# A block-sparse attention with a top-2 mixture of experts: eight key blocks per query block in f32, another order of the expert units, and seven block products in five experts' first layer

## The chip, the core and the metric

The kernel runs on one core of a Trainium2 chip. The core has TensorE (PE: matmuls, with weight loads beside them, PEld), VectorE (DVE), ScalarE (ACT), GpSimd (POOL) and SyncE (SP, which here issues DMAs). They share SBUF; matmuls write to PSUM, which DVE and ACT read. Each engine works through its own list in order and waits on semaphores for the others. The metric is device microseconds of one launch, the median of some runs.

## What is computed

```python
# attention: q, k, v (4 batches, 8 heads, 768 rows, 64 wide); blocks of 32 rows, so 24 blocks
mask = np.abs(blk_i - blk_j) <= 1                                  # neighbours
mask = mask | (blk_i == 0) | (blk_j == 0) | (blk_i == 23) | (blk_j == 23)   # first and last: all
mask[qb block, kb block] = True for kb in sampled_blocks[qb]       # three drawn blocks each
attn = softmax(where(mask, q @ k.T / 8, -1e9));  out = attn @ v
# experts: x = out as (3072, 512); 8 experts, 512 -> 1024 -> 512
noisy = x @ w_gate + log1p(exp(x @ w_noise)) * noise
top2, weights = two largest of noisy, softmax over the two
out[token] += weight * (relu(x[token] @ w1[e]) @ w2[e])            # for both experts of a token
```

So a query block outside the first and last sees at most eight of 24 key blocks: three neighbours, three drawn, two at the ends.

## The kernel before

**Attention** (class Attention, lines 46 to 423) computes dense scores. Two heads of a batch are a group; a step is one head and one tile of 128 rows, 192 steps in all. q and k are split into a high and a low f16 half (ACT copies, POOL subtractions in `split`), turned by DMA transposes, and the mask stands in extra rows of the operands. Per step PE runs two matmuls of 384 columns for the row maxima (`max_mm`, L227), four of 384 for the scores (`exp`, L255 and L256), and 18 of 64 or 65 columns for the product with v (`av`, L288: v in three f16 parts). DVE takes the row maximum over 768 scores (`max_red`, L234) and splits the exponentials, which ACT writes as integers (L257), into f16 halves (`halve`, L262). `steps` writes out the order by hand: within a step the pieces stand in a fixed order, maxima run a few steps ahead (`lead`), the product with v three steps behind (`LA`). The router's small operations stand between them (`background`).

**Routing** (class Router) runs per batch after its last group: it finds the two experts of each token and writes token number and weight into a table of slots in DRAM by indirect DMA.

**Experts** (class Experts) work in units: one of 640 rows for expert 0 (tokens of the first three batches), one of 224 rows for expert 0 (last batch), then seven of 816 rows for experts 1 to 7. A unit's rows are gathered from DRAM (POOL), turned by DMA (SP), and go through two layers with every operand split in two f16 halves, so three matmuls for one product. The first layer is `mm1` (L816; eight blocks of outputs, each 24 matmuls of up to 408 columns), ACT and DVE write the high and low halves of relu (L821, L822). The second layer is `mm2` (L836, 24 matmuls of 512 columns for 128 rows; L845 and the transposition L855 for the rows left over), then `finish` (L864: weight times result plus the token's earlier row) and an indirect DMA to `out` (L866). Weights come in eight pieces of 512 KB per expert (`load_piece` on SP's queue) and are split by ACT and DVE (`split_piece`, L729 and L730). `out` is filled with zeros during attention (`fill_out`, on ACT's queue).

The main function's loop over units says which loads, gathers and splits stand behind which block. Nothing is scheduled by a planner: the order on every engine is that of the code.

## Time and profile before

| | us |
|---|---|
| median of three runs | 1052.07 (1046.19 to 1056.2) |
| the profiled execution, its own span | 1028.6 |
| PE busy | 891.4 |
| DVE busy | 563.1 |
| ACT busy | 377.1 |
| POOL busy | 355.9 |

The span runs from the first to the last instruction that the profiler saw; the times of the runs hold something around it. Busy times are sums over stages with different limits, so they are read stage by stage. A matmul's duration holds a fixed part that the next one hides; the distance between two starts is what one costs in a row of them. "Granted clock" (PEclk) is TensorE's clock as a share of the full one.

### The profile page before, as it was taken

What the parts mean: (1) busy time and instruction counts of PE and PEld (TensorE: products, weight loads), DVE (VectorE), ACT (ScalarE), POOL (GpSimd) and SP (SyncE); (2) the same over time, 40 slices, a digit from 0 to 9 for tenths busy, and PEclk for the clock granted to TensorE, in tenths of its full rate; (3) what the DMA queues carried; (4) which work ended last, traced back from release to release, by engine and by line L of the source; (5) the groups of instructions that cost most, each with busy time, mean ns of one, the idle gap of its engine ahead of it and who ended that gap; (6) DMA issues with size and microseconds to landing.
All of it is one profiled execution on the core that took longest, in us unless ns stands there. A gap on an engine that the chain in (4) does not pass through costs nothing. (4 is left out here: it accounts for less than half of the span.)

```text
span 1028.6 us, 20575 instructions
## 1 busy us (share of the span) xinstructions
PE 891.4 (87%) x8413; PEld 529.1 (51%) x8413; DVE 563.1 (55%) x1039; ACT 377.1 (37%) x754; POOL 355.9 (35%) x399
## 2 busy tenths in 40 slices
PE   3788897779878878997899999989989999899993
PEld 1465565556555545653645455545544544454551
DVE  7699989979988977464123333323323323233320
ACT  2466666556656645432113123122122221221200
POOL 3142322542255253333360251342512513512211
PEclk9899999999999999998999999999999999999997
DMA  8988986899989766736957376295494483653200
GB/s 183 182 171 183 219 196 159 154 164 179 182 178 167 144 133 145 200 85 176 165 130 199 109 174 184 90 196 168 131 184 141 124 214 104 182 144 110 69 34 33
DMA packets 238073, 156.40 MB, mean 152 GB/s; under 512 B 172577, under 2 KB 213793, under 8 KB 237968
## 3 DMA queue, kind: packets, MB, share of 16 engines
q1 hardware_dynamic: 206816, 91.45, 44.1%
q0 software_dynamic: 14256, 39.58, 13.2%
q10 hardware_dynamic: 16896, 23.95, 8.6%
q8 instruction: 68, 1.11, 0.5%
q14 instruction: 37, 0.30, 0.1%
HBM read 79.62 MB, written 26.32 MB: 103 GB/s over the span
## 5 line engine op out<-in xcount | busy, mean ns | idle before, releaser
L257 ACT ACTIVATE p<-pe 128x384 int32<-128x384 f32 x384 | 183.0, 491 | 152.8 <-PE pe L256 125.7
L822 DVE SCALAR_TENSOR_TENSOR hl<-ph,hh 128x408 f16<-128x408 f32 (+2 forms) x136 | 75.6, 560 | 211.2 <-ACT hh L821 177.0
L866 POOL DMA_INDIRECT out_dram<-y,mt x56 | 73.0, 1304 | 323.9 <-DVE y L864 196.4
L234 DVE TENSOR_REDUCE m<-pm 128x1 f32<-128x768 f32 x192 | 181.6, 948 | 1.4 <-PE pm L227 1.4
L821 ACT ACTIVATE hh<-ph 128x408 f16<-128x408 f32 (+2 forms) x136 | 66.2, 492 | 301.9 <-PE ph L816 210.2
L227 PE MATMUL pm<-k,q 88*128 88x384 f16 x384 | 98.5, 340 | 67.8 <-DVE m L234 42.6
L262 DVE TENSOR_SCALAR p<-p 128x1536 f16<-128x1536 uint16 x192 | 124.7, 650 | 45.9 <-ACT p L257 44.0
L288 PEld LDWEIGHTS <-p 128*128 128x128 f16 x3456 | 130.4, 100 | 25.8 <-issue 4.7
L255 PE MATMUL pe<-q,k 128*128 128x384 f16 x384 | 128.7, 335 | 7.7 <-ACT p L257 4.4
L256 PE MATMUL pe<-q,k 128*128 128x384 f16 x384 | 127.9, 333 | 6.7 <-DMA q<-qb 6.7
L288 PE MATMUL po<-vx,p 128*128 128x65 f16 x1152 | 125.3, 197 | 1.8 <-issue 1.4
L288 PE MATMUL po<-vb,p 128*128 128x65 f16 x1152 | 125.8, 196 | 0.9 <-issue 0.9
L288 PE MATMUL po<-vl,p 128*128 128x64 f16 x1152 | 125.5, 195 | 0.0
L836 PEld LDWEIGHTS <-hh 128*128 128x128 f16 x768 | 75.0, 98 | 93.8 <-issue 8.8
L864 DVE SCALAR_TENSOR_TENSOR y<-py,mt,pv 128x512 f32<-128x512 f32 x48 | 36.0, 751 | 153.9 <-PE py L836 145.0
L816 PE MATMUL ph<-xta,w1hb 128*128 128x408 f16 x512 | 110.9, 339 | 9.6 <-DVE hl L822 8.7
L816 PE MATMUL ph<-xtb,w1ha 128*128 128x408 f16 (+1 forms) x448 | 95.3, 334 | 14.2 <-DVE hl L822 12.3
L227 PEld LDWEIGHTS <-q 88*128 88x128 f16 x384 | 37.9, 100 | 122.1 <-issue 96.7
L816 PEld LDWEIGHTS <-w1ha 128*128 128x128 f16 x576 | 57.4, 100 | 52.9 <-issue 18.4
L836 PE MATMUL py<-w2ha,hh 128*128 128x512 f16 x192 | 73.9, 385 | 4.9 <-DVE y L864 3.9
L816 PEld LDWEIGHTS <-w1hb 128*128 128x128 f16 x512 | 50.2, 98 | 49.7 <-issue 12.3
L836 PE MATMUL py<-w2la,hh 128*128 128x512 f16 x192 | 73.8, 384 | 0.3 <-issue 0.3
(172 smaller groups left out, 1404.3 us busy)
## 6 DMA issues: line engine op xcount, KB each, us to landing
wraw<-in_moe_w_dram SPq DMA_DIRECT2D x64, 512.0 KB
q<-q SPq DMA_DIRECT2D x32, 192.0 KB
raw_v<-in_v_dram ACTq DMA_DIRECT2D x16, 384.0 KB
out_dram<-zero ACTq DMA_DIRECT2D x8, 768.0 KB
x_rows<-x SPq DMA_DIRECT2D x16, 384.0 KB
raw_k<-in_k_dram ACTq DMA_DIRECT2D x14, 384.0 KB
raw_q<-in_q_dram ACTq DMA_DIRECT2D x14, 384.0 KB
k<-k SPq DMA_DIRECT2D x17, 192.0 KB
```

The lines of the kernel that those rows point to most:

```text
L227: self.nc.tensor.matmul(pm[:, c, 0:384], r["q3"][0:K, h, t, :], r["k2"][0:K, h, 3 * c:3 * c + 3, :], start=True, stop=True)
L234: self.nc.vector.tensor_reduce(self.st[g]["m", h][:, t:t + 1], pm[:, :, 0:384], axis=AX.XY, op=ALU.max)
L255: nc.tensor.matmul(pe[:, 0:384], r["k1"][:, h, c, :], r["q1"][:, h, t, :], start=True, stop=False)
L256: nc.tensor.matmul(pe[:, 0:384], r["k2"][:, h, c, :], r["q2", h][:, t, :], start=False, stop=True)
L257: nc.scalar.activation(p32[:, t].rearrange("p t c -> p (t c)"), pe[:, 0:384], AF.Exp, scale=0.125)
L262: self.nc.vector.tensor_scalar(p.rearrange("p t c w -> p (t c w)"), p32.bitcast(U16).rearrange("p t c -> p (t c)"), HC, None, op0=ALU.mult)
L288: self.nc.tensor.matmul(o, p[:, t, :, w], v, start=first and i == 0, stop=last and i == 2, skip_group_check=True)
L816: nc.tensor.matmul(ph[:, b, 0:m], w[wt][:, kb, fs], r["xt"][:, kb, a, o:o + m], start=i == 0, stop=i == last)
L821: nc.scalar.activation(hv, ph[:, b, 0:m], AF.Relu)
L822: nc.vector.scalar_tensor_tensor(self.hl[:, f, o:o + m], ph[:, b, 0:m], 0.0, hv, op0=ALU.max, op1=ALU.subtract)
L836: nc.tensor.matmul(py, h[:, f, o], w[x][:, f, :], start=i == 0, stop=i == last)
L866: nc.gpsimd.indirect_dma_start(out=self.out, out_offset=bass.IndirectOffsetOnAxis(ap=r["mt"][0:m, c, 0:1], axis=0), in_=y[0:m], in_offset= ...
```

## The change

**Inputs** are laid out on the host: q and k turned (two heads on 128 partitions), v with its columns in groups of four, v's rows of each query block's neighbours side by side (`vw`), weights in the order of the new pieces.

**Attention** works on f32 without splits. A q item is one batch, one tile of 128 query rows and four heads; there are 48. For each query block of 32 rows (`j`) and each head its scores are one matmul of 32 rows by 192 key columns (three neighbours in place, three drawn blocks that POOL has copied beside them with a block number from a register), and one per head for the 64 columns of the two end blocks. The two heads of a pair sit on partitions 0 to 63 and 64 to 127, the four query blocks write to strips of 32 partitions. DVE takes maxima, ACT the exponentials, PE turns them in f32, DVE and ACT copy them out, and 32 matmuls of 68 columns multiply with v, whose rows SP loads by block number. Repeated blocks get weight zero through `known`. A g item takes the first and the last query block of two heads against all keys; there are 16. x is turned by PE (`turn_x`) and no longer by DMA.

**Order of units:** 640 rows for experts 0 and 1 (first three batches), then 224 rows for experts 1 and 0 (last batch), then 816 rows for experts 2 to 7. Units 0 and 2 write `out` without reading it. `fill_out` stands in unit 0's first layer, on SP's queue.

**Experts 3 to 7** compute the first layer from seven products of blocks in place of eight (`layer1_fast`, 28 products in four groups of seven): sums of weight blocks (`weight_sums`, DVE) and of row blocks (`row_sums`, `row_differences`, DVE) are formed one unit ahead, and the products are added on the way out of PSUM (ACT copies, DVE additions). PSUM has seven single banks in place of three pairs.

The core of the diff:

```diff
-    def exp(self, n, x):
-        nc.tensor.matmul(pe[:, 0:384], r["k1"][:, h, c, :], r["q1"][:, h, t, :], start=True, stop=False)
-        nc.tensor.matmul(pe[:, 0:384], r["k2"][:, h, c, :], r["q2", h][:, t, :], start=False, stop=True)
-        nc.scalar.activation(p32[:, t].rearrange("p t c -> p (t c)"), pe[:, 0:384], AF.Exp, scale=0.125)
+    def scores(self, it):
...
+            for kh in range(2):
+                for e in range(2):
+                    mm(s[kh][64 * e:64 * e + 64, 0:384], qg[h, 2 * i + e, :],
+                       kk[h, NB // 2 * kh:NB // 2 * kh + NB // 2, 2 * i + e])
...
+        for e in range(2):
+            p = 2 * f + e
+            for j in range(self.NJ):
+                blk = min(max(t * self.NJ + j - 1, 0), NB - 3)
+                for par in range(2):
...
+                    mm(s[par][32 * j:32 * j + 32, e, 0:192], q[head(par), p, 32 * j:32 * j + 32], w)
+        for e in range(2):
+            p = 2 * f + e
+            for par in range(2):
+                mm(s[par][:, e, 192:256], q[head(par), p, :], kk[head(par), 0:NB:NB - 1, p])
+    def soft(self, it):
...
+        for par in range(2):
+            nc.vector.tensor_reduce(m[:, par], s[par].rearrange("p (e c) -> p e c", e=2), axis=AX.X, op=ALU.max, negate=True)
+        for par in range(2):
+            for e in range(2):
+                nc.scalar.activation(p[:, 2 * e + par], s[par][:, 256 * e:256 * e + 256], AF.Exp, bias=m[:, par, e:e + 1])
+    def av(self, it):
...
+        for h in range(4):
+            for x, v in ((0, va), (1, vb)):
+                for j in range(self.NJ):
+                    nc.tensor.matmul(o[32 * j:32 * j + 32, h], d[:, h % 2, h // 2, x, 32 * j:32 * j + 32],
+                                     self.values(v[:, self.slot(t, j)], 4 * f + h), start=h == 0 and x == 0,
+                                     stop=h == 3 and x == 1, skip_group_check=True)
+    def prefetch_k(self, b, t):
...
+        v = self.numbers(self.ri, t, mybir.EngineType.Pool, self.NB - 1)
...
+        for j in js:
+            for n in range(3):
+                nc.gpsimd.tensor_copy(kk[:, self.row(t, j) + n], flat[:, bass.ds(v[j, n] * P, P)])
+    def prefetch_v(self, b, t):
...
+        nc.sync.dma_start(va[0:96, js[0]:js[-1] + 1, 0:HD], part(self.vw[b, t]))
...
+        for j in js:
+            for n, d in enumerate((va[96:128, j], vb[0:32, j], vb[32:64, j])):
+                nc.sync.dma_start(d[:, 0:HD], vv[bass.ds(v[j, n], 1)].rearrange("o p c -> (o p) c"))
-        self.units = [(0, 0, CA), (E, 0, CB)] + [(e, e, C) for e in range(1, E)]
+        self.units = [(0, 0, CA), (1, 1, CA), (E + 1, 1, CB), (E, 0, CB)] + [(e, e, C) for e in range(NH, E)]
+    def layer1_fast(self, u, hook):
...
+        for n, (g, p) in enumerate(PRODUCTS):
...
+            for s in range(2):
+                for wt, a in ((0, 0), (0, 1), (1, 0)):
+                    nc.tensor.matmul(o, w[:, wt, slot, s * P:s * P + P], mv(s, a), start=i == 0 and p in tail,
+                                     stop=i == 5, skip_group_check=True)
...
+            if p == 2:
+                tt(once[g], bc[:, 0:M], once[g])
+                self.high(g, 0, M, once[g])
+                later.append((g, 0, M, once[g]))
+            if p == 4:
+                tt(both[g][:, 0], bd[:, 0:M], both[g][:, 0])
+            if p in (5, 7) and {(g, 5), (g, 7)} <= seen:
+                tt(both[g][:, 1], ba[:, 0:M], both[g][:, 1])
```

Three places show what stands on the engines. First PE within a step of attention: the two score matmuls of one half, two for a maximum of a later step, and the first of the 18 with v (p are the exponentials, vx, vl and vb the parts of v). Before:

```order
L227 LDWEIGHTS q_1413
L227 MATMUL pm<-k_101,q_1413 128x384
L255 LDWEIGHTS k_913
L255 MATMUL pe<-q_1074,k_913 128x384
L256 LDWEIGHTS k_100
L256 MATMUL pe<-q_1636,k_100 128x384
L288 LDWEIGHTS p_1789
L288 MATMUL po<-vx_103,p_1789 128x65
L288 LDWEIGHTS p_1789
L288 MATMUL po<-vl_109,p_1789 128x64
```

One q item of the change (ps holds scores and then the turned p, kk the keys, ptr the turned p in SBUF; va holds neighbours and the first drawn block, vb the rest):

```order
L298 MATMUL ps<-r_ident,p 128x128 x8
L225 MATMUL ps<-kk_105,q 32x192 x16
L225 MATMUL ps<-kk_105,q 128x64 x4
L320 MATMUL po<-va_99,ptr 32x68 x4
L320 MATMUL po<-vb_102,ptr 32x68 x4
```

The L320 pair stands four times, once for each head; outputs are now strips of 32 partitions. In the built program each of these f32 matmuls but the transpositions is two weight loads and two matmuls, which the list does not show.

Second, DVE in attention. Before, about once a step:

```order
L262 TENSOR_SCALAR p_4721<-p_4691 128x1536
L234 TENSOR_REDUCE m<-pm 128x1
L543 RECIPROCAL r_iw<-r_w 128x48
L546 SCALAR_TENSOR_TENSOR r_r_4757<-r_w,r_u 128x48
L262 TENSOR_SCALAR p_4759<-p_4726 128x1536
```

and in the change, once a q item:

```order
L302 COPY ptr<-ps 128x512
L391 COPY r_xT<-po 128x1024
L271 TENSOR_REDUCE m<-ps 128x2 x2
L327 TENSOR_SCALAR rc<-po 128x4
L328 RECIPROCAL rc<-rc 128x4
L330 TENSOR_TENSOR xr<-po,rc 128x256
```

The conversion over 1536 is gone and the maxima are over 512 scores in place of 768; r_ names are the router's.

Third, DVE in an 816-row unit's first layer. Before it held little but the low halves (hl) of relu and some weights:

```order
L822 SCALAR_TENSOR_TENSOR hl<-ph,hh 128x408 x4
L730 SCALAR_TENSOR_TENSOR w2la<-wraw,w2ha 128x1024
L752 TENSOR_SCALAR gi<-mt 128x6
L752 TENSOR_SCALAR gi<-mt 48x1
L822 SCALAR_TENSOR_TENSOR hl<-ph,hh 128x408 x12
```

and in a fast unit of the change (ta and tc are the sums of products, pa, pc and pd the PSUM banks, xf the row sums of the next unit):

```order
L963 SCALAR_TENSOR_TENSOR hl<-tc,hh 128x816
L963 SCALAR_TENSOR_TENSOR hl<-ta,hh 128x408
L825 SCALAR_TENSOR_TENSOR w_9985<-wraw,w_9985 128x1024
L836 TENSOR_TENSOR xf<-xta 128x816
L980 TENSOR_TENSOR tc<-pd,tc 128x408
L963 SCALAR_TENSOR_TENSOR hl<-pa,hh 128x408
L836 TENSOR_TENSOR xf<-xta 128x816
L980 TENSOR_TENSOR tc<-pa,tc 128x408
```

Additions that free a PSUM bank now stand in one list with sums for the next unit.

## Rows read from the trace of the kernel before

**Rows 1.** The page: span and busy time of the engines.
```profile
span 1028.6 us, 20575 instructions
PE 891.4 (87%) x8413; PEld 529.1 (51%) x8413; DVE 563.1 (55%) x1039; ACT 377.1 (37%) x754; POOL 355.9 (35%) x399
```

**Rows 2.** Stretches: length, busy us (count) by engine, granted clock, DMA share, GB/s.
```profile
11.00:420.00 409.00, 333.93 (x4777) 227.71 (x4777) 355.96 (x679) 239.76 (x535) 154.93 (x191) 0.97 0.85 172
420.00:514.00 94.00, 79.44 (x585) 50.03 (x583) 39.24 (x103) 26.37 (x46) 36.08 (x46) 0.93 0.66 156
514.00:1012.00 498.00, 477.98 (x3056) 251.18 (x3054) 158.80 (x231) 106.95 (x167) 160.12 (x141) 0.99 0.53 140
1012.00:1028.60 16.60, 0.00 (x0) 0.00 (x0) 0.64 (x1) 0.00 (x0) 0.98 (x1) 0.65 0.05 19
...
405.00:420.00 15.00, 11.83 (x203) 9.09 (x200) 5.92 (x11) 7.41 (x19) 3.82 (x4) 0.89 0.93 202
```

**Rows 3.** Groups by line in attention (busy us, mean ns, idle before), PE's longest wait.
```profile
L234 DVE TENSOR_REDUCE m<-pm 128x1 f32<-128x768 f32 x192 | 181.6, 948 | 1.4 <-PE pm L227 1.4
L262 DVE TENSOR_SCALAR p<-p 128x1536 f16<-128x1536 uint16 x192 | 124.7, 650 | 45.9 <-ACT p L257 44.0 <-issue 1.0
L257 ACT ACTIVATE p<-pe 128x384 int32<-128x384 f32 x384 | 183.0, 491 | 152.8 <-PE pe L256 125.7 <-PE pm L227 7.5 <-remote 7.0
...
PE pm L227 <- DVE m L234: 42.6, 79, 1.6
```

**Rows 4.** Timeline of PE in the experts: start us, length us, engine, line, operation.
```profile
516.35 0.85 PE L816 MATMUL ph<-xta,w1hb 128*128 128x408 f16 x4
...
582.92 0.38 PE L836 MATMUL py<-w2hb,hh 128*128 128x512 f16 x1
583.14 0.38 PE L836 MATMUL py<-w2lb,hh 128*128 128x512 f16 x1
...
439.75 0.71 PE L816 MATMUL ph<-xta,w1ha 128*128 128x320 f16 x4
```

**Rows 5.** Timeline of PE and its weight loads in one step of attention.
```profile
203.10 0.74 PEld L288 LDWEIGHTS <-p 128*128 128x128 f16 x18
...
203.97 0.32 PE L256 MATMUL pe<-q,k 128*128 128x384 f16 x1
204.13 0.49 PE L227 MATMUL pm<-k,q 88*128 88x384 f16 x2
```

**Rows 6.** The f32 transposition: one instance in the timeline; durations ns min/median/max.
```profile
990.53 0.60 PE L855 MATMUL pr<-r_ident,yt 128*48 128x128 f32 x4
...
L855 PE MATMUL pr<-r_ident,yt x32: 272/273/273, 513.7 to 990.9; 128*48 128x128 f32 x28, 128*96 128x128 f32 x4
```

**Rows 7.** Groups by line and shape on DVE and ACT.
```profile
L822 DVE SCALAR_TENSOR_TENSOR hl<-ph,hh 128x408 f16<-128x408 f32 x112 | 64.8, 582 | 188.1 <-ACT hh L821 160.8 <-issue 27.3
L822 DVE SCALAR_TENSOR_TENSOR hl<-ph,hh 128x224 f16<-128x224 f32 x8 | 3.0, 390 | 14.6 <-ACT hh L821 8.1 <-issue 6.4
L305 DVE RECIPROCAL rc<-rc 128x6 f32<-128x6 f32 x32 | 5.8, 180 | 0.0
...
L849 ACT ACTIVATE yt<-py 128x192 f32<-128x192 f32 x7 | 2.3, 330 | 38.7 <-PE py L845 32.3 <-PE pr L937 6.4
```

**Rows 8.** POOL's groups by line and shape; one DMA issue on SP's queue.
```profile
L317 POOL TENSOR_TENSOR x<-xr,x 128x384 f16<-128x384 f32 x32 | 29.8, 931 | 22.4 <-ACT x L315 22.3
L647 POOL DMA_INDIRECT slots<-r_pay,r_sl x48 | 51.5, 1072 | 39.4 <-DVE r_ot L639 30.2 <-issue 7.7 <-DVE r_pay L636 1.2
...
1.70 0.42 SPq L330 DMA_DIRECT2D raw_q<-in_q_dram  x1
```

**Rows 9.** Timeline of PE in the first two units, with waits in brackets.
```profile
478.97 0.59 PE L836 MATMUL py<-w2ha,hh 128*128 128x512 f16 x1 [3.63 <-DVE y L864]
...
501.47 0.53 PE L816 MATMUL ph<-xtb,w1ha 128*128 128x224 f16 x2 [3.66 <-DVE hl L822]
```

More of the change, by code (lines that the diff above doesn't have):

```diff
@@ L36 @@
 CB = 224
-NV = E + 1
+NH = 2
+NV = E + NH
 OVT = 18
@@ L163, in vsplit @@
-    def vsplit(self, g, part):
-        nc, D = self.nc, self.D
-        r = self.st[g]
-        vh, vl, vb = r["v"]
-        vh, vb = vh[:, :, :, 0:D], vb[:, :, :, 0:D]
+        self.ps_g = pool(ctx, "ps_g", 1, space=PSUM)
+        ep = pool(early, "aeb", 1)
+        two = lambda n: ep if n == 2 else self.buf
+        J = self.NJ
+        self.va = [two(i).tile([P, J, self.HW], F32, name=f"va{i}") for i in range(3)]
+        self.vb = [two(i).tile([P, J, self.HW], F32, name=f"vb{i}") for i in range(3)]
@@ L587, in run @@
         nc.scalar.activation(ex, dl, AF.Exp)
-        for _ in range(self.YL if last else self.YN):
+        for _ in range(self.YL if last else self.YN + 8 * (b == self.B - 2)):
             yield
@@ L598, in run @@
                          skip_group_check=True)
-        for _ in range(self.HO):
+        for _ in range(self.HO if last else 0):
             yield
@@ L779, in gather_prev @@
         r = self.st["u", u]
-        for c in self.chunks(u):
+        for c in () if self.plain(u) else self.chunks(u):
             m = self.rows_of(u, c)
@@ L796, in rows_of, with layer1 @@
         return P if c < full else left
+    def layer1(self, u, hook):
+        nc = self.nc
+        self.hh = self.hp.tile([P, self.FB, C], F16, name="hh")
+        self.hl = self.hp.tile([P, self.FB, C], F16, name="hl")
+        if self.fast(u):
+            return self.layer1_fast(u, hook)
+        for n, f in enumerate(FORDER):
+            self.mm1(u, f)
+            hook(n)
     def mm1(self, u, f):
@@ L833, in mm2 @@
             i = 0
-            for f in range(self.FB):
-                for h, x in ((self.hh, "w2h"), (self.hh, "w2l"), (self.hl, "w2h")):
-                    nc.tensor.matmul(py, h[:, f, o], w[x][:, f, :], start=i == 0, stop=i == last)
+            for f in FORDER:
+                for h, x in ((self.hh, 0), (self.hh, 1), (self.hl, 0)):
+                    nc.tensor.matmul(py, h[:, f, o], w(f)[:, x], start=i == 0, stop=i == last)
                     i += 1
@@ L1025 @@
     ip = early.enter_context(tc.tile_pool(name="init", bufs=1))
-    zero = ip.tile([P, DM], F32, name="zero")
+    zero = rp.tile([P, 256], F32, name="zero")
+    nc.vector.memset(zero, 0.0)
     att.start(ip)
-    nc.gpsimd.memset(zero, 0.0)
-    at(18, router.blank_table, ip)
-    at(21, router.send_table)
-    att.steps(on_group, step)
+    at(7, router.blank_table, ip)
+    at(9, router.send_table)
+    att.steps(router, done, step)
     late.close()
     ex.open_right(right)
+    second = ExitStack()
@@ new lines, in do @@
+    def do(u, what):
+        e = ex.units[u][1]
+        while freed:
+            next_load(*freed.pop(0))
+        for op, *a in what:
+            if op == "h":
+                ex.high_piece(e + (a[0] < 4), a[0])
+            elif op == "l":
+                low(e + (a[0] < 4), a[0])
+            elif op == "s":
+                if u + 1 < nu:
+                    ex.weight_sums(e + 1, a[0])
+            elif op in ("g", "x"):
+                v = u + (1 if a[0] < 0 else 2)
+                c = abs(a[0]) - (a[0] < 0)
+                if v < nu and v > FAST:
+                    (ex.gather if op == "g" else ex.xpose)(v, c)
+            else:
+                {"rs": ex.row_sums, "rd": ex.row_differences, "rh": ex.row_high, "rl": ex.row_low}[op](u + 1, *a)
```

1215 lines of the change are left out of this document (694 added, 521 removed), and 5 rows, old and new, of the table BACK.

## The prediction

> **What bounds the kernel now.** The stages come first, from the table of stretches [rows 2]. The profiled execution (span 1028.6 us [rows 1]) has four parts: 11.0 us until matmuls run in numbers, attention to 420, the first two expert units (640 and 224 rows) to 514, seven units of 816 rows to 1012, and a tail of 16.6 us. The median of the runs shown is 1052.1 us, 23.5 above the span; I carry that difference over unchanged.
>
> In attention VectorE (DVE) is busy 356 of 409 us and TensorE (PE) 334. The grouped lines name DVE's work: 192 row maxima of 948 ns and 192 conversions of 650 ns, 306 us; PE's longest wait there is for such a maximum, 42.6 us in 79 waits [rows 3]. So DVE holds attention, with PE close behind. In the seven expert units PE is busy 478 of 498 us and DVE 159: PE holds them, 498 / 7 = 71.1 us each.
>
> What a matmul costs is read from distances between starts, since matmuls overlap. Four of 408 columns take 0.85 us and one lasts 0.33, so starts are 0.171 apart; 512 columns 0.215, 320 columns 0.137 [rows 4]. That is one column per cycle of 2.4 GHz; the fixed 0.17 us of each duration is hidden in a row of matmuls. Weights of 128 columns load every 0.041 us (18 in 0.74 [rows 5]). The one f32 work on PE is the transposition of yt: four of 128 columns in 0.60, one lasts 0.273, so 0.109 apart [rows 6]: two cycles a column.
>
> **Attention after.** The dense scores, row maxima and conversions go. Now 48 q items (four heads, 128 queries, eight key blocks of 32 for each query block) and 16 g items (first and last query block against all keys) run, all in f32. In the built program an f32 product is two weight loads and two matmuls, one for either half of the weights; a transposition is one of each. No row shows such a product. Bounds: one pass at the transposition's two cycles a column, or two such passes. I take two, as the program has them: 192 columns cost 2 x 0.160 us.
>
> The second unknown weighs more. Consecutive matmuls now use different rows or columns of the array (heads on partitions 0 to 63 and 64 to 127, outputs in strips of 32). No row of before has two of them on the array at once; all its matmuls use 88 rows or more. Bounds: nothing overlaps, or all do. I take the middle case: both passes of one matmul need the same part of the array and the engine's order is kept, so a matmul's second pass lies beside the next one's first, and n matmuls cost n + 1 passes in place of 2n. Per batch (without overlap in brackets):
> - scores: 12 items x 17 passes x 0.160 = 32.6 us (12 x 32 x 0.160 = 61.4)
> - keys of the end blocks: 8 passes with 128-column weights, by the loads 8 x 0.041 = 0.33, x 12 = 4.0 (5.1)
> - transpositions of p: 12 x 8 x 0.109 = 10.5 (same)
> - product with v: 32 matmuls of 68 columns, 33 passes x 0.057, x 12 = 22.6 (43.8)
> - g items: 4 x (5 x 0.320 + 8 x 0.109) = 9.9 (13.7); their product with v 65 x 0.057 = 3.7 (7.3)
> - transpositions of x in f16, by DMA before: 48 x 0.055 = 2.6 (same).
>
> Sum 85.9 us a batch (144.4), four batches 344, the router's 56 matmuls a batch about 7 in all. The start stays at 11: the first g item needs the keys of one batch, 1.57 MB, 9 us at the 172 GB/s of [rows 2]. Attention ends at 11 + 344 + 7 = 362 in place of 420: -58.
>
> The Trainium skill, page "TensorEngine Tiling (Array Packing)", section "Tiling Modes", says that a change of tile shape drains the engine. By it, 62 changes a batch at the hidden 0.17 us would add 43 us. The trace does not settle it: an 88-row matmul follows a full one 0.16 later, without a gap [rows 5], and no smaller shape ran. The forecast leaves it out.
>
> What else must stay under PE's 85.9 / 12 = 7.2 us an item? DVE: reading PSUM costs 0.157 us + 1.04 ns an element (582 ns at 408, 390 at 224 [rows 7]). Two maxima of 512: 1.38; ptr copy 0.69; norm 0.18 + 0.18 [rows 7] + 0.42; half a turned x 0.61; a third of a g item 0.65; the router, an estimate of 30 us in all, 0.6. That is 4.7. ACT: four exps of 256 at 0.39 (330 ns at 192, 491 at 384 [rows 3, 7]), a copy 0.60, high 0.39: 2.6. POOL, per tile of two items (14.4 us): a scaling 1.2, two low 1.2, table writes 2.1, and eleven copies of 128 columns between nearly nothing and the 0.93 of a 384-column subtraction [rows 8]: 4.6 to 14.8; the copies are a third as wide, so I take 8. SP: 13 v loads and four more issues at 0.42 [rows 8], 7 us a tile. Without this cover each us over 14.4 would cost 24 us. DMA: v 34.6 MB, q, k and the rows of x 6.3 each, 53.5 MB in 351 us is 152 GB/s, below the 172 moved now. All hidden.
>
> **Expert units after.** At full rate 816 rows cost 192 x 0.171 (first layer, two halves of 408) + 144 x 0.215 (second) + 96 x 0.020 (the 48 rows left over) + 0.4 = 66.1 us, where 71.1 was measured: 5.0 lost a unit. A unit of 640 costs 192 x 0.137 + 120 x 0.215 = 52.1; one of 224 about 96 x 0.093 + 24 x 0.215 + 96 x 0.040 + 0.4 = 18.3. Before, these are 70.4 where 94.0 was measured, so 23.6 lost, among it waits of 3.6 us for y and 3.7 for hl [rows 9] and a clock of 0.93 [rows 2]. After there are two of each, 140.8. The last batch's routing now has 104 us of cover and not 52, but the zero fill of out (6.3 MB) has moved from attention into unit 0, ahead of weights on SP's queue. I take 15 lost: bounds 5 (a full unit's), and 32 (12.6 MB of fills, weights and rows at 202 / 0.93 = 217 GB/s [rows 2] need 58 us where the first layer takes 26).
>
> Then one plain unit, 71.1, and five fast ones. Seven block products for eight: 28 x 6 = 168 matmuls of 408 in place of 192, 24 x 0.171 = 4.1 less, 67.0 each. Their DVE work grows, by the formula above: sums from PSUM 12 x 0.58, lows 8 x 0.58 + 4 x 1.0, weights 4 x 1.22 + 4 x (0.96 + 1.22), weight sums 16 x 0.42, row sums and differences 12.3, y 5.3: 53 us a unit where 159 / 7 = 23 stood. It fits under 67 by little; I take no loss. Sum 140.8 + 15 + 71.1 + 335 = 562, before 592: -30.
>
> **Sum.** 362 + 562 + 16.6 = 940.6, plus 23.5 = **964 us**, own range 930 to 1000.
>
> **Rivals.**
> - Changes of tile shape cost a drain each, 4 x 62 x 0.17 = 43 more: 1007. For it: five shapes alternate in every item. Against: nothing in the rows. Chance 0.20. (The Trainium skill's rule in "TensorEngine Tiling (Array Packing)", section "Tiling Modes", is this one; no run here shows it.)
> - The fast units wait for DVE. In their first layer DVE has 26 us of work within 28.9 and stands between the PSUM banks and PE. If each loses 8: 40 more, 1004. Chance 0.09.
> - More overlap, or a cheaper f32 pass: PE falls below DVE. 4.7 x 48 = 226 us at the 0.87 share that DVE reaches now [rows 2] is 260, attention ends near 274: 876. Chance 0.13.
> - Slower: matmuls on different parts of the array do not overlap. Attention ends at 4 x 144.4 + 18 = 596: 1198. For it: nothing in the trace runs two at once. Against: the program alternates the parts. The point that decides: with the rest as above, attention must end before 450, 108 us a batch, so 62% of the assumed overlap is needed. Chance 0.12.
> - Slower: the clock. It was 0.97 in attention, 0.93 in the broken stretch to 514 [rows 2]. If narrow f32 matmuls ran at the lower level of 1.2 GHz, 344 would double: 1308. Chance 0.04.
>
> That the change doesn't do what it says is no rival: the dense steps are gone from the program.
>
> **How the numbers follow.** Forecast 0.42, drains 0.20, DVE 0.09, more overlap 0.13, no overlap 0.12, clock 0.04. The range 870 to 1060 holds the first four with their spread and leaves out the last two and some edges. A measurement of this kernel tells about 1% from no change. Faster by over 1% (below 1041): 0.41 + 0.15 + 0.06 + 0.13 = 0.75; within 1%: 0.01 + 0.04 + 0.02 = 0.07; slower: 0.01 + 0.01 + 0.16 = 0.18.
>
> **What would show it.** PE's starts within an item's scores 0.16 apart per matmul: the forecast; 0.32: no overlap; under 0.1: more overlap. Gaps of 0.1 to 0.2 us ahead of each change of shape: drains. The first expert matmul near 362, fast units 67 us apart, PE waiting for tc, ta or hl under 3 us a unit. The prediction is wrong in its reasons if PE is idle over a tenth of attention, or if DVE is the busier engine there.

## The result and the profile after

The changed kernel takes 918.87 us (median, 910.61 to 930.65) against 1051.28 (1046.19 to 1056.2) for the kernel before, run beside it: a ratio of 0.8758, 95% interval 0.8671 to 0.8845. (The run of 930.65 us came in a slower state of the core, and the ratio leaves it out.) The forecast was 964 us, range 870 to 1060. So the direction and the range held, but the point lies 45 us too high, outside the 930 to 1000 that the forecast gave its own mechanism and about as far from it as from its rival "more overlap" (876). Several of its steps were wrong, two of them in ways that cancel. The profiled execution took 920.24 us with a span of 918.2.

The page of the changed kernel, its head, beside [rows 1]:

```profile
span 918.2 us, 25196 instructions
...
PE 825.8 (90%) x10119; PEld 520.8 (57%) x10119; DVE 538.0 (59%) x1151; ACT 357.5 (39%) x666; POOL 381.3 (42%) x662
...
q8 instruction: 81, 1.33, 0.7%
```

The last line is one of the DMA queues: 81 packets, 1.33 MB, so 16 KB each. It returns below.

Stretches of the changed kernel, with the columns of [rows 2]: attention, the two units of 640 rows, the two of 224, the plain unit of 816, the five fast units, the tail.

```profile
14.00:353.67 339.67, 286.87 (x6485) 218.37 (x6486) 201.85 (x565) 168.07 (x373) 171.96 (x470) 0.90 0.71 170
353.67:462.30 108.63, 107.49 (x680) 62.94 (x680) 44.39 (x111) 27.69 (x51) 34.22 (x44) 0.98 0.71 206
462.30:511.50 49.20, 43.26 (x442) 34.99 (x441) 12.80 (x35) 10.36 (x22) 16.36 (x15) 0.90 0.59 143
511.50:586.67 75.17, 69.42 (x438) 36.11 (x436) 45.20 (x67) 21.34 (x31) 35.38 (x26) 0.95 0.76 182
586.67:902.14 315.47, 315.23 (x2062) 167.04 (x2060) 224.89 (x335) 125.12 (x185) 119.02 (x92) 1.00 0.53 143
902.14:918.20 16.06, 0.00 (x1) 0.00 (x0) 0.75 (x1) 0.00 (x0) 0.98 (x1) 0.64 0.06 20
```

Attention ends at 353.67 where it ended at 420 [rows 2] (forecast 362). The experts take 548.5 us to the last matmul (forecast 562; 592 before). The five fast units are 63.0 us each, PE busy without a break. DVE, which held attention before, is busy 202 of 340 us there. PE is the busiest, but idle 53 of 340, and its granted clock is 0.90 there.

PE's waits in attention, 14 to 350 us (total, times, longest):

```profile
PE po L320 <- issue: 23.9, 43, 2.4
PE ps L225 <- issue: 6.3, 6, 3.5
PE pog L346 <- issue: 6.3, 14, 1.3
PE po L390 <- DVE xe L369: 4.1, 4, 2.0
PE po L662 <- DVE xr L330: 4.0, 3, 1.9
```

36.5 of 53 us are "issue": PE stands in the middle of a row of matmuls and waits for nothing that the profile names. Here is one undisturbed q item, PE's timeline (start, length):

```profile
150.49 1.09 PE L298 MATMUL ps<-r_ident,p 128*128 128x128 f32 x8
151.51 1.47 PE L225 MATMUL ps<-kk,q 64*32 64x192 f32 x40
152.92 0.33 PE L320 MATMUL po<-va,ptr 128*32 128x68 f32 x8
153.06 0.30 PE L320 MATMUL po<-vb,ptr 128*32 128x68 f32 x8
153.18 0.30 PE L320 MATMUL po<-va,ptr 128*32 128x68 f32 x8
```

All 40 score passes are through in 1.41 us (152.92 - 151.51), and eight passes with v start every 0.12 us, so 64 in 0.94. Transpositions, scores and product come to about 3.4 us, 162 us for 48 q items; attention, with 16 g items, the turned x and the router's matmuls, takes 340. The item just ahead shows one reason:

```profile
147.49 0.30 PE L320 MATMUL po<-va,ptr 128*32 128x68 f32 x8
147.81 0.33 PE L320 MATMUL po<-vb,ptr 128*32 128x68 f32 x4
148.55 0.22 PE L320 MATMUL po<-vb,ptr 128*32 128x68 f32 x1 [0.41 <-issue]
149.28 0.22 PE L320 MATMUL po<-vb,ptr 128*32 128x68 f32 x1 [0.51 <-issue]
150.01 0.28 PE L320 MATMUL po<-vb,ptr 128*32 128x68 f32 x2 [0.52 <-issue]
```

The product with v, 0.94 us when it runs through, takes 3.3 us here, in bursts 0.73 us apart. So attention has far less work than the forecast gave it, and loses time in a way that the forecast did not hold.

**Two patterns of stalls.** I counted PE's recorded instructions (matmuls, weight loads and the semaphore instructions between them) from the first one on. In the first 100 us the three longest waits without a named releaser stand behind number 1216, 1728 and 1984; in other executions behind 704, 2240, 2752, 3264, 4544, 4800. The differences are multiples of 256, on all three chips named below. Of these instructions 20412 are on record, and the instruction queue brought 81 packets: one per 252. So a block of 16 KB holds 256 of PE's instructions, and these are waits for the next block. The packets' own times agree: with the changed kernel on the quick chip (below) 14 of the 15 such waits of over 0.4 us in attention, 24.4 us, end 1.2 to 1.6 us after a packet of this queue has landed. In the first profile it is 11 of 47, 13.7 us. The second pattern is the train above: short bursts 0.7 us apart. It has another place: 37 of those 47 waits begin within 2.3 us after one of the 36 writes by which POOL fills the slots in attention (L716), and such times are 19% of attention (a few waits count for both).

### The profile page after: what moved, and what is told of

The parts are those of the page before. It is cut to its first block, busy times and chain, and to the rows that moved or that the text cites. A ratio compares the mean times of both kernels' runs of the same rounds, so it can differ in the third digit from the quotient of the medians.

```text
span 918.2 us, 25196 instructions
## 1 busy us (share of the span) xinstructions
PE 825.8 (90%) x10119; PEld 520.8 (57%) x10119; DVE 538.0 (59%) x1151; ACT 357.5 (39%) x666; POOL 381.3 (42%) x662
## 3 DMA queue, kind: packets, MB, share of 16 engines
q0 software_dynamic: 13760, 38.01, 13.2%
q8 instruction: 81, 1.33, 0.7%
## 4 chain that ended last, share of the span: by engine, by line
PE 81%; issue 6%; DVE 6%; another core or an unknown queue 2%; ACT 1%; DMA 1%; POOL 0%; SPq 0%; DVEq 0%; POOLq 0%
PE pc L1038 27%; PE ps L225 10%; PE pa L991 9%; PE po L320 7%; PE ps L298 5%; PE pa L952 5%; PE pd L991 5%; PE pd L952 3%; PE pc L1047 3%; PE pog L346 2%; PE pc L991 2%; DVE m L271 2%; PE ps L286 2%; PE po L390 1%
## 5 line engine op out<-in xcount | busy, mean ns | idle before, releaser
L1038 PE MATMUL pc<-w,hh 128*128 128x512 f16 x768 | 229.5, 380 | 0.0
L1038 PE MATMUL pc<-w,hl 128*128 128x512 f16 x384 | 146.0, 380 | 0.0
L991 PEld LDWEIGHTS <-w 128*128 128x128 f16 x840 | 82.2, 98 | 63.1
L274 ACT ACTIVATE p<-ps,m 128x256 f32<-128x256 f32 x192 | 75.2, 474 | 73.7 <-DVE m L271 63.8
L271 DVE TENSOR_REDUCE m<-ps 128x2 f32<-128x512 f32 x96 | 61.9, 684 | 49.8 <-PE ps L225 42.9
L225 PE MATMUL ps<-kk,q 64*32 64x192 f32 (+1 forms) x1920 | 75.9, 333 | 7.1 <-issue 6.3
L894 POOL DMA_INDIRECT xg<-x_rows,gi x56 | 69.9, 1249 | 23.4 <-issue 15.0
L320 PE MATMUL po<-va,ptr 128*32 128x68 f32 x1536 | 61.5, 237 | 16.8 <-issue 12.7
L186 POOL COPY kk<-kk 128x128 f32 x264 | 64.6, 295 | 28.2 <-PE ps L225 21.6
L825 DVE SCALAR_TENSOR_TENSOR w<-wraw,w 128x1024 f16<-128x1024 f32 (+1 forms) x58 | 65.2, 1126 | 18.9 <-ACT w L821 18.9
L320 PE MATMUL po<-vb,ptr 128*32 128x68 f32 x1536 | 63.4, 234 | 11.5 <-issue 11.2
L716 POOL DMA_INDIRECT slots<-r_pay,r_sl x48 | 48.7, 1014 | 39.2 <-DVE r_pay L705 27.3
L320 PEld LDWEIGHTS po<-va,ptr 128*32 128x32 f32 x1536 | 41.5, 115 | 31.0 <-issue 19.2
```

Source lines behind the costliest of these rows:

```text
L186: nc.gpsimd.tensor_copy(kk[:, self.row(t, j) + n], flat[:, bass.ds(v[j, n] * P, P)])
L225: mm = lambda o, l, r: nc.tensor.matmul(o, l, r, start=True, stop=True, skip_group_check=True)
L271: nc.vector.tensor_reduce(m[:, par], s[par].rearrange("p (e c) -> p e c", e=2), axis=AX.X, op=ALU.max, negate=True)
L274: nc.scalar.activation(p[:, 2 * e + par], s[par][:, 256 * e:256 * e + 256], AF.Exp, bias=m[:, par, e:e + 1])
L320: nc.tensor.matmul(o[32 * j:32 * j + 32, h], d[:, h % 2, h // 2, x, 32 * j:32 * j + 32], self.values(v[:, self.slot(t, j)], 4 * f + h), st ...
L825: self.nc.vector.scalar_tensor_tensor(lo, t, WS, hi, op0=ALU.mult, op1=ALU.subtract)
```

## The experiments

Three chips took part, and the kernel before ran at 996.44, 1036.06 and 1051.95 us (medians) on them; I call them the quick, the middle and the slow one. Which chip gave the first result above is not on record; the times of the kernel before beside it are those of the slow one. Comparisons in microseconds are made on one chip, or say so. On the middle chip the kernel before spread over 1028.66 to 1044.28 us and the four ratios carry no verdict; the changed kernel itself did not run there, and the readings rest on the traces.

**Without v's traffic** (middle chip).

```diff
     def prefetch_v(self, b, t):
...
+        if b * self.T + t >= 3:
+            return
...
```

> The loads of v after the first three tiles are left out (30 of 34.6 MB), with whatever waits for them; the product with v reads what the three buffers hold, so its numbers are of other rows. The changed kernel's attention runs from 14 to 350 us; in it TensorE is idle 51 us, 36.5 of them in rows of matmuls that wait for nothing the profile names (issue), in bursts of a few matmuls with 0.4 to 0.7 us between. Theory A, instructions: the profile's instruction queue carries 81 blocks of 16 KB against 20238 matmuls and weight loads, one per 250, and such a block comes late while v is on the DMA engines: the issue waits fall from 36.5 to under 8 us and attention ends by 320, the whole 30 or more shorter. Theory B, late v: the same gain, but by v itself. Theory C, the chain of an item (PE, DVE maximum, ACT exponential, PE) sets the pace: attention ends at 340 or later whatever the issue waits do, since other waits take their place.

Measured: 888.22 us (886.08 to 892.12), ratio to before 0.8619 [0.8568, 0.8669]; attention ends at 328.8, with 22.3 us of issue waits left.

**v loaded but not read** (middle chip). `av` and `global_av` read buffer 0; the loads go to buffers 1 and 2.

```diff
-        va, vb = self.st["v", b, t]
+        va, vb = self.va[0], self.vb[0]
...
```

> All loads of v are made, but into two buffers that nobody reads; the product with v reads a third one, loaded once, so its numbers are of other rows and nothing waits for a later load. Theory A (instruction blocks come late behind the traffic of v): the issue waits stay near 36 us and attention ends at 343 to 360. Theory B (v itself is late): as without loads, attention ends by 320. Theory C: no change, ends at 340 to 355 with the issue waits as they come.

Measured: 911.45 us, 0.8834 [0.8777, 0.8891]; attention ends at 344.1, issue waits 34.1. So with the traffic but without any wait for v, the stalls are all there; without the traffic attention is 15 us shorter. That speaks for the traffic (A) and against late v (B) and a chain that sets the pace whatever happens (C). But theory A had named under 8 us and an end by 320, and 22.3 us stay without traffic, mostly trains: A is not all. Sorted by place, the waits of over 0.4 us that end after a packet landed fall from 16.3 to 2.1 us when v is not loaded; of the 24 that are left 20 stand behind POOL's writes.

PE's waits with v not loaded (its lines stand two further down):

```profile
PE po L322 <- issue: 16.9, 34, 1.1
PE pog L348 <- issue: 4.6, 14, 0.5
```

None is longer than 1.1 us now: the long block waits are gone, the short bursts are not.

**Same part of the array in a row** (middle chip). The loops change places, so that eight products of one strip follow each other in the product with v, and two of one part in the scores.

```diff
...
-        for h in range(4):
-            for x, v in ((0, va), (1, vb)):
-                for j in range(self.NJ):
+        for j in range(self.NJ):
+            for h in range(4):
+                for x, v in ((0, va), (1, vb)):
```

> The same matmuls in another order: consecutive score matmuls (two heads pairs of one block) and consecutive products with v (eight of one block) now use the same part of the array, where the change alternates the parts. In the changed kernel 40 score passes take 1.41 us and 64 passes with v 0.95 us an item. If the overlap comes from alternating parts: 32 x 0.160 + 0.33 = 5.4 us and 64 x 0.057 = 3.6 us, and 48 items make attention some 150 to 310 us longer, the span 1070 to 1230. If passes overlap whatever part they use: 1.4 and 0.95 as now, span within 10 of 918. The forecast's own model (a second pass beside the next matmul's first) would lie at 3.0 and 1.9 with alternating parts, and gives the long version here.

Measured: 958.94 us (958.52 to 959.35), 0.9291 [0.9233, 0.935]; attention ends at 396.8. One item of it:

```profile
143.74 1.53 PE L225 MATMUL ps<-kk,q 64*32 64x192 f32 x40
145.20 0.31 PE L320 MATMUL po<-va,ptr 128*32 128x68 f32 x2
145.34 0.28 PE L320 MATMUL po<-vb,ptr 128*32 128x68 f32 x2
145.46 0.28 PE L320 MATMUL po<-va,ptr 128*32 128x68 f32 x2
145.57 0.28 PE L320 MATMUL po<-vb,ptr 128*32 128x68 f32 x2
...
145.93 0.31 PE L320 MATMUL po<-va,ptr 128*32 128x68 f32 x4
...
148.27 0.28 PE L320 MATMUL po<-vb,ptr 128*32 128x68 f32 x2
```

With v, two passes start every 0.117 us where eight did: 0.0585 a pass, no overlap within a strip, against the 0.057 of the forecast's formula. Only where one strip follows another do passes overlap (the rows of four), so the whole product takes 3.13 us where it took 0.94. So the overlap of the change is fourfold and comes from the four strips alternating. The scores did not slow down: two products in a row in one part, with eight parts in turn, still take 1.46 us. That half of the expectation was wrong; what order of the scores would break their overlap was not tried.

More telling is the total. 48 items x 2.2 us is 106 us more work on PE, but attention ended only 53 us later than with v unread on this chip (and not 150 to 310). PE's idle time fell from 52 to 22 us, issue waits among it from 34.1 to 10.9 with a single one left behind a packet, and the clock rose from 0.93 to 0.99: a slower PE hardly outruns its instructions.

```profile
14.00:396.00 382.00, 360.94 (x6485) 305.96 (x6486) 200.07 (x564) 168.66 (x372) 170.87 (x468) 0.99 0.62 151
```

**The zero fill of `out` in attention** (middle chip).

```diff
+    for i in range(8):
+        at(40 + i, fill_out, i)
...
-            fill_out(f)
```

> The eight fills of out (6.3 MB) move from the first layer of unit 0 to attention's items 40 to 47, one an item, on the same queue. In the changed kernel unit 0 takes 68 us (350 to 418) at a DMA share of 0.94 and 279 GB/s, where full rate is 52. If the fills hold its weights and rows up: unit 0 takes 52 to 57, attention ends within 4 us of now, the span falls by 8 to 15. If unit 0 is held by the splitting of weights on ACT and DVE, or by its gathers: it stays above 64 and the span within 5. If the added traffic makes attention's issue waits longer: attention ends 5 to 15 later and takes the gain back.

Measured: 916.55 us (911.16 to 921.66), 0.8863 [0.8796, 0.8931]. The 68 us in this expectation was a misreading of mine (it was the width of a window): from its first matmul to the next unit's, unit 0 takes 55.35 us in the changed kernel, and 56.1 here. The fills did not hold it up. Attention ends at 357.7 with 43.3 us of issue waits, later than with v unread on this chip (344.1); what of that the fills add is not shown, as the changed kernel did not run here.

**The changed kernel on the quick chip.**

> The changed kernel itself, beside the three others on one chip, to have its attention's end, its waits and its fast units there: attention ends at 345 to 355, issue waits of TensorE in it 33 to 40 us, fast units 63.0 us each.

Measured: 890.62 us (885.45 to 892.78), 0.8927 [0.885, 0.9003]. Attention ends at 340.5, with 26.4 us of issue waits, fast units 63.0. There are no trains here, only single long waits at multiples of 256. PE also waits 5.7 us for rows of v. There is another wait instead:

```profile
PE ps L225 <- POOL q L166: 11.0, 2, 10.3
```

Attention of this execution:

```profile
14.00:340.00 326.00, 268.11 (x6485) 208.07 (x6486) 202.04 (x565) 167.59 (x372) 170.61 (x468) 0.93 0.74 175
```

The place of the wait for q, on PE and (second fence) on POOL, the same execution:

```profile
286.88 1.09 PE L298 MATMUL ps<-r_ident,p 128*128 128x128 f32 x8
298.25 2.58 PE L225 MATMUL ps<-kk,q 64*32 64x192 f32 x40 [10.27 <-POOL q L166]
```

```profile
295.29 0.97 POOL L716 DMA_INDIRECT slots<-r_pay,r_sl  x1 [0.22 <-issue]
296.25 0.09 POOL L715 MEMSET r_spacer<- 1x1 f32 x1
296.56 0.97 POOL L716 DMA_INDIRECT slots<-r_pay,r_sl  x1 [0.22 <-issue]
297.55 0.64 POOL L166 TENSOR_SCALAR q<-q 128x512 f32<-128x512 f32 x1
```

The scaling of q stands in POOL's list behind eleven of the third batch's twelve slot writes, 1.3 us each with the memset and the issue, and twelve copies of keys. PE waits 10.3 us; the scores after that pause take 2.58 us in place of 1.47. The granted clock of 250 to 300 us is 0.84, between its two levels, 0.5 (1.2 GHz) and 1. In the first profile the wait for q is 0.8 us.

**Without the slot writes of the first three batches** (quick chip). L716 is left out for them.

> The 36 writes of the first three batches' slots (indirect DMAs that GpSimd issues, L716) are left out, so the first units work on empty slots; nothing else changes, the small memset beside each stays. In the runs so far the rows of AV matmuls that wait for nothing named lie at 132 to 172, 218 to 257 and 287 to 307 us, where these writes lie, also without v traffic, with about 0.7 us from one short burst of matmuls to the next. Theory D, the writes hold TensorE up: these trains vanish, TensorE's issue waits in attention fall by 15 us or more below the unchanged kernel's, and attention ends 12 to 25 us sooner. Theory A (instruction blocks alone): the trains stay where they are, waits within 5 us, attention within 4 us.

Measured: 865.69 us (862.2 to 867.29), 0.869 [0.8617, 0.8762]. Attention ends at 316.6, 23.9 us sooner; the wait for q is gone, issue waits are 19.4. So the writes cost this chip 24 us, the size that theory D named, but its mechanism is not seen here: there are no trains on this chip, and the issue waits fell by 7 us, not 15. The largest single piece is the wait behind POOL's list, 11 us; another 7 is PE's busy time, at a clock of 0.95 for 0.93:

```profile
14.00:316.00 302.00, 260.77 (x6485) 202.91 (x6486) 202.04 (x565) 167.59 (x372) 134.79 (x432) 0.95 0.72 188
```

**Without the slot writes and without v's traffic** (quick chip).

> As the kernel without the slots' writes, and the loads of v after the first three tiles left out as well, so the product with v reads rows of other tiles. If both are causes of their own, their gains add up: attention ends 35 to 50 us sooner than in the unchanged kernel and issue waits fall below 6 us; what is left of the 337 us is then the chain of an item and the work. If the chain of an item sets the pace after either, the two together gain less than 30 us.

Measured: 831.08 us (829.9 to 832.26), 0.8343 [0.8258, 0.8428]. Attention ends at 281.1, 59.3 us sooner than in the changed kernel, more than the 35 to 50 expected, and 35.5 sooner than without the writes alone. Issue waits are 2.0 us. The two gains do not eat each other up; whether they just add is not shown, since the kernel without v alone did not run on this chip (on the middle one v's traffic cost 15 us). Beside the pair the chain of an item costs little: PE is busy 93% of attention.

```profile
14.00:281.00 267.00, 247.56 (x6485) 194.03 (x6486) 200.61 (x565) 166.86 (x373) 136.88 (x435) 0.99 0.35 102
```

```profile
121.93 1.47 PE L227 MATMUL ps<-kk,q 64*32 64x192 f32 x40
124.42 1.09 PE L300 MATMUL ps<-r_ident,p 128*128 128x128 f32 x8
125.44 1.47 PE L227 MATMUL ps<-kk,q 64*32 64x192 f32 x40
...
129.48 0.61 PE L392 MATMUL po<-a_ident,x 128*128 128x128 f16 x8
130.02 1.47 PE L227 MATMUL ps<-kk,q 64*32 64x192 f32 x40
```

Two items with their turned x, one tile, take 8.09 us (130.02 - 121.93). This is the pace of the matmuls themselves; the forecast's terms for the same work come to 12.0 (its 14.4 a tile hold the g items too).

Attention from 14 us to its end, in us, with the granted clock (a share of 2.4 GHz):

| kernel, chip | length | PE idle | of it issue | PE busy | clock |
|---|---|---|---|---|---|
| changed, first profile | 339.7 | 52.8 | 36.5 | 286.9 | 0.90 |
| v unread, middle | 330.1 | 52.0 | 34.1 | 278.1 | 0.93 |
| v not loaded, middle | 314.8 | 40.6 | 22.3 | 274.2 | 0.95 |
| same part in a row, middle | 382.8 | 21.8 | 10.9 | 361.0 | 0.99 |
| changed, quick | 326.5 | 58.4 | 26.4 | 268.1 | 0.93 |
| no slot writes, quick | 302.6 | 41.8 | 19.4 | 260.8 | 0.95 |
| neither, quick | 267.1 | 19.6 | 2.0 | 247.6 | 0.99 |

So a wait costs twice. In the three kernels on the quick chip the matmuls of attention are the same, but PE is busy 20.6 us longer in the changed one than in the last. TensorE's clock falls to 1.2 GHz after pauses (the scores behind the pause of 10.3 us took 2.58 us in place of 1.47), for 46 us of attention in the changed kernel and 8 in the one with neither; by the scores' ratio those 38 us more cost up to 17 (an estimate). The rest of the 59.3 us is idle time: 24.4 less of issue waits, 11.0 for q, 5.7 for v, and 2 more for others.

**Eight products again in experts 3 to 7** (quick chip): `fast` returns False, no sums.

> Experts 3 to 7 back to eight products in the first layer (192 matmuls of up to 408 columns in place of 168), with the sums of weights and rows left out; everything else as in the change. At 0.171 us a matmul the forecast's step says 4.1 us more a unit, 67.1 in place of 63.0 at the same loss, 20.5 us over five units. If the units of before had lost their 5.0 us to something that the new order of loads does not cure: 71.1 each, 40 us longer. If the sums on VectorE cost the fast units time that plain units do not pay: under 66 each, less than 15 us longer.

Measured: 900.79 us (899.44 to 904.74), 0.9052 [0.8978, 0.9126]: 10.2 us more than the changed kernel. The plain unit and the next one, first with seven products, then with eight:

```profile
486.87:558.92 72.05, 68.89 (x438) 36.20 (x436) 45.20 (x67) 21.45 (x31) 35.30 (x26) 0.98 0.79 190
558.92:621.91 62.99, 62.99 (x414) 33.40 (x412) 49.81 (x73) 27.03 (x39) 28.77 (x22) 1.00 0.67 170
```

```profile
480.17:547.22 67.05, 67.05 (x438) 35.66 (x436) 24.33 (x33) 15.29 (x25) 32.23 (x26) 1.00 0.83 208
547.22:614.28 67.06, 67.06 (x438) 35.72 (x437) 22.78 (x31) 15.30 (x25) 25.58 (x21) 1.00 0.60 164
```

A fast unit saves 4.06 us, the forecast's 4.1 exactly. But the plain unit ahead of them is 5.0 us longer, as it prepares the sums for the first fast one. Over all units the gain is 15.1 us (548.6 - 533.5, first to last expert matmul); attention, which the edit leaves alone, was 6 us shorter in this execution, so single profiles tell no smaller difference there. In the changed kernel's plain unit on this chip DVE shows a reason for 3 of the 5 us: a row sum waits for transposed rows, the low half hl stands behind it, and PE waits for hl.

```profile
517.30 1.01 DVE L836 TENSOR_TENSOR xf<-xtb 128x816 f32<-128x816 f16 x1 [6.96 <-DMA xtb<-xg]
518.23 0.57 DVE L963 SCALAR_TENSOR_TENSOR hl<-pa,hh 128x408 f16<-128x408 f32 x1
```

```profile
PE pd L952 <- DVE hl L963: 3.2, 1, 3.2
```

**The changed kernel on the slow chip.**

> The changed kernel itself, for comparison with the three others on the same chip. Fast units 63.0 us, attention's length and its issue waits as this chip has them (36.5 us and an end at 353.7 on the first chip, about 25 and 340.5 on the last).

Measured: 918.3 us, 0.8723 [0.8669, 0.8777]; attention ends at 348.2, issue waits 32.5.

**The last batch's q not sooner** (slow chip).

```diff
-            ... (nq > self.late_) == (new[3] == 1):
+            ... new[3] == 0:
```

> The loads of the last batch's q go back to the tile's first item, one item later than in the change; nothing else differs. If the load was on the path: a wait of TensorE or of GpSimd for q, and attention ends 2 to 10 us later. If other work covers it, as the forecast held (it priced this edit at nothing): attention's end and the time within 4 us of the changed kernel's.

Measured: 916.91 us, 0.873 [0.8685, 0.8776], attention ends at 350.4, issue waits 37.8, PE's wait for q is 0.8 us in both: no difference that can be told. This part of the change is hidden, as forecast.

**v's loads in quarters** (slow chip).

```diff
-        nc.sync.dma_start(va[0:96, js[0]:js[-1] + 1, 0:HD], part(self.vw[b, t]))
...
         for j in js:
+            nc.sync.dma_start(va[0:96, j:j + 1, 0:HD], ...[:, j:j + 1])
```

> The one load of 768 KB that opens each tile's v becomes four of 192 KB, each ahead of its block's three loads of 64 KB: same bytes, three issues more a tile, but at most 0.4 MB are handed to the DMA engines within 2 us where 0.9 MB are now. If TensorE's instruction blocks wait behind what is already queued (theory A): the issue waits in attention fall by a third or more (10 us) and attention ends 6 to 15 us sooner than in the changed kernel. If they suffer from the traffic as such (busy share 0.7): waits within 5 us, attention within 5 us. If SyncE's queue becomes late by three more issues of 0.4 us: attention ends 5 or more later, with waits for v.

Measured: 912.18 us, 0.8674 [0.863, 0.8718]; issue waits 24.9 (32.5 in the changed kernel beside it), attention ends at 347.7. The waits fell by a quarter, but attention is the same within 1 us, and the two intervals overlap. Inconclusive: if a shorter queue helps, it is by less than these runs tell. The waits of over 0.4 us behind a packet hardly changed, 10.4 us for 11.5, and they are those that theory A meant.

**Three edits together** (slow chip): quarters, fewer slot writes an item, row sums later in the plain unit.

> A try at a better kernel, three edits: v's loads in quarters as in the run above; the third batch's slot writes two or three an item in place of five or six, so that the scaling of q on GpSimd does not stand behind eleven of them (TensorE waited 10.3 us for it once); and in the unit ahead of the fast ones the next unit's row sums two to three blocks later, since they waited 7.0 us for transposed rows and held the low halves up, TensorE 3.2. Expected: the q wait under 2 us, attention 5 to 10 us sooner than in the run above; the plain unit 67.5 to 69 in place of 72.1; together 8 to 14 us below the run above. If the writes' wait turns up elsewhere (gathers of the first unit begin later): the attention's gain is lost in unit 0, which then takes 62 or more in place of 56.

Measured: 912.01 us, 0.8665 [0.8621, 0.8709]. It is no candidate: four of the third batch's slot writes now come behind the read of the first unit's slots, so the first units lack rows. What can be read is the plain unit, whose work is whole: 70.8 us in place of 75.15 beside it, so the later row sums seem to be worth about 4 us. Less than that is shown: three more executions with the old place (the first profile and the two runs above) took 75.1 to 75.5, but on the middle chip the same unit took 70.0 to 74.6 with no edit to it. Attention ends at 345.0 (348.2), 2.7 us sooner than in the run above and not 5 to 10, and the whole is no shorter than that run. No kernel here beats the changed one by more than the measurement tells.

## Why the forecast was right in range, and where its steps failed

**Bottleneck.** The forecast named a test of its reasons: wrong if PE is idle over a tenth of attention. It was idle 53 of 340 us, 16%. So attention's end, off by only 8 us (353.7 for 362), came out by luck, by two errors of opposite sign: PE was busy 287 us where the forecast had 351, and idle 53 where it had nothing.

**First error: the overlap.** Two passes at two cycles a column was right (0.0585 a pass with v when nothing overlaps). The step that failed is "n matmuls cost n + 1 passes". It gave 3.05 us for the scores with the end-block keys and 1.88 for the product with v; they take 1.41 and 0.94. All four strips run at once in the product with v, not two neighbours. The scores, with eight parts in turn, gain no more: 1.41 us is 3.8 times less than the 5.4 without overlap. The Trainium skill, page "TensorEngine Tiling (Array Packing)", section "Tiling Modes", says that different tiles can load weights and multiply in parallel, and lists 128x32 as four tiles. The trace agrees: four times 0.0146 us a pass alternating is 0.0585. I had used one property from that list, the drain, and not the one beside it. Without v's traffic and the slot writes attention ended at 281 us on the quick chip; the rival "more overlap" had put it at 274. But it had DVE hold attention then, and PE is the busier one there too (248 us for 201).

**Second error: "all hidden".** The forecast gave DMA 152 GB/s and called it hidden because each load had time. It had 170 at a busy share of 0.71. The loads themselves were nearly in time (in the first profile PE waits for none of v, on the quick chip 5.7 us), but PE's instructions are DMA traffic too. An item has 224 matmuls and weight loads in 3.4 us of work: nearly a block of 256 per item. With v's traffic blocks are late. On the quick chip, with the slot writes left out, v's traffic costs 35.5 us: 17.4 of issue waits, 6.6 of waits for v and 13.2 of longer busy time, at a clock of 0.95 for 0.99. The Trainium skill, page "Runtime: NRT & Kernel Launch", section "Instruction fetch mechanics", has the 256 instructions in 16 KiB and calls the cost of such a boundary mostly hidden. The trace agrees with the block, and with the second only by number: of 51 blocks in the changed kernel's attention on the quick chip 14 made PE wait over 0.4 us, up to 4.3 each, 24.4 us together; it was 2 of 51 and 2.0 us in the kernel without v's traffic and slot writes. Why a block is late, whether its request comes late or waits behind other traffic, stays open.

**Third: POOL's list.** The forecast summed POOL's time per tile (8 us of 14.4; measured 172 us in 24 tiles, 7.2) and called it hidden. The sum was right. It missed that the writes come in clumps: eleven between one scaling of q and the next. The writes cost 24 us on the quick chip, 11 of them in this wait; in the first profile the wait is 0.8 us, and the writes' part there is not shown.

**Right in the small.** DVE's and POOL's prices from formulas and bounds held, but for the turned x, whose f16 copy is cheaper (0.69 for 1.22), and the scaling of q on POOL (0.62 for 1.2). ACT's exponentials took more, 0.474 for 0.39:

```profile
L186 POOL COPY kk<-kk 128x128 f32 x264 | 64.6, 295 | 28.2 <-PE ps L225 21.6 <-issue 3.9 <-DMA vb<-in_vx_dram 1.9
L271 DVE TENSOR_REDUCE m<-ps 128x2 f32<-128x512 f32 x96 | 61.9, 684 | 49.8 <-PE ps L225 42.9 <-remote 6.8
L391 DVE COPY r_xT<-po 128x1024 f16<-128x1024 f16 x24 | 16.5, 686 | 5.3 <-PE po L390 3.3 <-issue 1.3
```

Two maxima at 0.684 are the 1.38 of the forecast; a copy of keys takes 0.295, between its bounds of nothing and 0.93.

**Rivals.** Drains: not decided. Eight transpositions 0.109 apart fill 0.87 of the 1.02 us until the scores start, so this change of shape costs at most about 0.15 us; no run separates a drain from other causes, and it is part of the 8.09 us a tile. DVE in the fast units: PE never waited there; DVE was busy 49.8 to 50.0 us in each of the first four (forecast 53). No overlap did not come. The low clock came in part: 0.90 over attention, some 65 of 340 us at 1.2 GHz, and 0.99 in the kernel where PE hardly waited. By the scores' 2.58 us for 1.47, an estimate of what that cost is up to 28 us; the forecast had put it at nothing, and it came with PE's pauses, not with narrow matmuls as such.

**Experts.** The first four units took 157.8 us (353.67 to 511.50), forecast 155.8; that it held the fills as the reason was wrong, since moving them did not shorten unit 0. Of the 17.0 us over full rate 12.6 lie in the two units of 224 rows, at a clock of 0.90. On the quick chip these two take 18.99 each and all four lose 5.6, so the 15 of the forecast was met by luck; why they differ stays open. The plain unit took 75.2 for 71.1: row sums that wait for rows, a wait the forecast did not look for in that unit. The fast units took 63.0 for 67.0: the product count was right to 0.04 us, but I carried over the 5.0 us that a unit of before lost over full rate, and now a fast unit loses about 1 (63.0 against 62.0), as a plain one does where no sums are formed (67.05 against 66.1, eight products again). Five times 4 us: the largest error among the experts. The new order of the units was not undone on its own.

**The carry of 23.5 us.** This was half of the miss (21.5 of 43.8 us), and it was no property of the kernel. In every run here the time is about 2 us above its span. Before's profile came from an execution as the middle chip gives them (1028.66 to 1044.28), the times shown from one as the slow chip does (1042.5 to 1055.89). The difference between slow and quick chip is 55.5 us for the kernel before and 27.7 for the changed one, with the fast units at 63.0 on both. In the changed kernel it sits in attention (7.7 us) and in the units ahead of the five with seven products (17.8), so it does not carry over as a constant.

In numbers for the profiled execution: attention -8.3, experts -13.5, tail -0.5, carry -21.5, together -43.8, from 964 to 920.2.

## What to carry to other kernels

Small matmuls that take turns on different parts of the array can overlap well beyond neighbours, fourfold here with four strips and no more with eight parts; but then count instructions, since an engine that gets through 256 of them in 4 to 5 us can wait for the next block when the DMA engines are loaded (14 of 51 blocks at a busy share of 0.74, 2 of 51 at 0.35). A pause can cost twice, as the clock may be lower behind it (2.58 us in place of 1.47 behind a pause of 10.3). An engine's list wants its order checked, not only its sum: a row of small writes ahead of one operand cost 10 us. And a difference between a profile's span and a median from elsewhere is first a difference between executions and chips, before it is an overhead to carry over.

## What the runs showed of the hardware

- TensorE slower by 106 us of added work cost 53 us of time, since it then idled less (21.8 us for 52.0, issue waits 10.9 for 34.1) and kept a higher clock (0.99 for 0.93).
- A wait for a block of 256 instructions ends 1.2 to 1.6 us after its 16 KB packet has landed (14 waits, quick chip).
- The trains of short bursts are not explained. On the slow and the middle chip they stand where POOL writes slots: in the first profile 37 of 47 issue waits of over 0.4 us begin within 2.3 us after one of the 36 writes, in 19% of the time. On the quick chip it is 1 of 15, with the same writes. The kernel without writes ran on the quick chip alone, so whether the writes cause the trains elsewhere stays open.
- The same program took 890.6 and 918.3 us on two chips, the kernel before 996.4 and 1052.0.
